# Attention's first group of q and k assembled by ScalarE instead of SBUF transfers, and the constant rows of the second buffer copied by a transfer

## The chip, the cores and the metric

The kernel runs on one core of a Trainium2 chip. A core has TensorE (PE, with its weight load PEld), VectorE (DVE), ScalarE (ACT), GpSimd (POOL) and SyncE (SP), which run their own instruction queues in order and wait for each other through semaphores. Transfers are issued by SP, ScalarE or GpSimd and carried by 16 DMA engines. The metric is device time in microseconds of one execution; lower is better. The times before are three runs, and one further execution was profiled.

## What is computed

The reference computes causal attention with a bias for 8 batches of 8 heads (576 positions, 64 wide), and sends each of the 4608 rows through one of 8 experts with a capacity of 576 rows each.

```python
scores = scale * np.matmul(q, k.transpose(0, 1, 3, 2))
s_pos = np.maximum(s, 0.0)
cum = np.cumsum(s_pos, axis=-1)
bias = -(cum[:, :, :, None] - cum[:, :, None, :])
scores = np.where(causal, -1000000000.0, scores + np.minimum(bias, 0.0))
scores = scores - np.max(scores, axis=-1, keepdims=True)
attn = np.exp(scores)
attn = attn / (np.sum(attn, axis=-1, keepdims=True) + 1e-09)
return np.matmul(attn, v).astype(np.float32)
...
x = np.ascontiguousarray(attn_out.transpose(0, 2, 1, 3)).reshape(B * S, H * D)
return _moe_ref(x=x, **moe_kwargs)
```

## The kernel before

Attention takes the first 309 us of the profiled execution; routing and the experts follow and depend on all of it. The 64 heads are worked on in 16 groups `g` of four heads. A group has two passes `pr`, and a pass two heads `par`, so there are 32 passes `n0 = 2*g + pr`.

Each group has one of four `QK` buffers, 128 partitions by two planes by q and k by two passes by 1280 columns. Values are carried in fp16 twice: `hi`, the scaled value rounded to fp16, and `lo`, what the rounding left. In plane 0, partitions 0 to 63 hold `hi`; partitions 64 to 69 are six extra rows with constants, the digits of the cumulated bias ("aux", line 416) and the row maxima. Plane 1 holds `hi` and `lo` one above the other on 128 partitions. `load` (line 384 on) builds a group:

- two loads each of q and k into `raw` (line 401), of which there are two buffers; the next group but one can be loaded when `raw` has been read;
- `hi` by ScalarE (line 428) and `lo` by VectorE (line 430), each on 128 partitions, into plane 1;
- six pieces `q2`, `k2`, `q3`, `k3`, `q4`, `k4` and two `e1` that bring 64-partition halves to the other half or plane. `move` (line 435) does this by a transfer from SBUF to SBUF of 72 KB for each pass; for the first group `e1` is a ScalarE activation from `raw` (line 438). The first group is done in two parts, one for each pass: 4 `e1` and 12 transfers.

The passes of a group then go through these steps:

- `spass` ("bound pass"): nine units of matmuls into `pss` (lines 505, 521; three PSUM buffers), each followed by a masked maximum on VectorE into `mr` (line 490). When all nine are done, two small activations (537, 539), a GpSimd subtraction (541), a transposition on TensorE (544) and an activation (546) make `mt`, and a transfer of 5 KB (549 on SP, 550 on ScalarE's queue) writes the maxima into partitions 67 and 68 of `QK`.
- `sts` ("score pass"): seven units of matmuls into `pst` (564 to 567, 607 to 609), the exponential by ScalarE (575) into `P`, and what bf16 leaves of it by GpSimd (577) into `R`. Its units need the maxima's transfer and all six pieces.
- `pv` (642 to 644): 90 small matmuls with V into `po`; then VectorE and ScalarE normalise (671, 675, 687 to 691), and `turn` transposes for the router (725, 744).

`consts` fills the six extra rows of all four `QK` buffers ahead of time: VectorE writes those of the buffers 0 and 1 (line 304), and GpSimd starts a transfer from buffer 1 to the buffers 2 and 3 (line 309).

The order of instructions is not written out. Every step is a task with an engine, an assumed duration, what it depends on and a priority `prio`. `Plan.run` is a list scheduler: over and over it takes, on the engine that is free first, the ready task of the lowest `prio`, by assumed durations, and emits it. A changed number thus moves instructions on all engines. The first `WARM` tasks on TensorE are matmuls on zeros (line 795, priority 50), which fill time until real ones are ready.

Of the kernel before, what the change touches and what calls it, by code (L numbers as in the profile page):

```python
# [27 lines left out]
QS = 32.0  # L28
# [10 lines left out]
PW = 1536  # L39
WARM, HALF = 70, 4  # L40

# [188 lines left out]
class Attention:  # L230
# [35 lines left out]
    def consts(self):  # L266
# [31 lines left out]
        for i in range(4):  # L298
            t = self.r["QK"].slots[i][0]
            p0 = -97 if i == 0 else 2 * i - 5.6  # L300
            rows, made = t[64:70, 0], []
            if i < 2:
                for c in (1, 0):
                    made.append(pl.add("v", 0.85, lambda rows=rows, c=c: nc.vector.tensor_scalar(
                        rows[:, c].rearrange("p r (h c) -> p (r h) c", h=2), zrow, self.vec[64:70, c:c + 1], None,
                        op0=OP.add), [k["vec", 0, 4], k["vec", 1, 1], k["mZ"]], prio=p0 if c or i else -94, lock=True))
            else:
# [4 lines left out]
            k["row", i] = made  # L312
            if i == 1:
                self.rows1, self.moved = made, []
# [67 lines left out]
    def load(self, g):  # L382
# [41 lines left out]
        for a, z in parts:  # L424
# [3 lines left out]
            hi = [pl.add("a", dur, lambda t=t, a=a, z=z: act(part(A_, 1, t, t, a, z), raw.t[:, t, a:z], AF.Copy, scale=QS),  # L428
                         [ld[r, t] for r in range(a, z)], prio=t0 - 5 + off + t / 10, uses=[raw, QK]) for t in range(2)]
            lo = [pl.add("v", 0.15 + n * S / 960, lambda t=t, a=a, z=z: stt(  # L430
                part(A_, 1, t, 1 - t, a, z), raw.t[:, t, a:z], QS, part(A_, 1, t, t, a, z), op0=OP.mult,
                op1=OP.subtract), [hi[t]], prio=t0 - 4.648 + off + t / 10, uses=[raw, QK], lock=True) for t in range(2)]

# [7 lines left out]
            else:  # L441
                e1 = [move((E_, 0, t, 0), (E_, 1, t, t), hi[t:t + 1], -4.4 + t / 20) for t in range(2)]
            q2 = move((E_, 0, 0, 1), (O_, 1, 0, 0), hi[:1], -4.3)
            k2 = move((E_, 0, 1, 1), (O_, 1, 1, 1), hi[1:], -4.25)
            q3 = move((O_, 1, 0, 0), (E_, 1, 0, 1), [lo[0], q2], -3.8)
# [7 lines left out]
    def vload(self, g):  # L453
        nc, pl, k = self.nc, self.pl, self.k
        b, hf = divmod(g, 2)
        t0, st = 2 * g, self.st[g]
        rv, V, Vl = self.buf("rv"), self.buf("V"), self.buf("Vl")
        st.update(V=V, Vl=Vl)
        ld = [pl.add("s", 0.45, lambda r=r: nc.sync.dma_start(rv.t[:, r], self.vN[b, :, 2 * hf + r]), prio=t0 - 4.5, uses=[rv],
                     kb=295, bulk=True) for r in range(2)]  # L460
        hi = pl.add("a", 0.2 + 2 * S / 1200, lambda: nc.scalar.activation(V.t[:, :, :, 0:64], rv.t, AF.Copy, scale=VS),
                    ld + ([k["V", g]] if g < 3 else []), prio=t0 - 1.852, uses=[rv, V])
        lo = pl.add("v", 0.15 + 2 * S / 960, lambda: nc.vector.scalar_tensor_tensor(
            Vl.t, rv.t, VS, V.t[:, :, :, 0:64], op0=OP.mult, op1=OP.subtract), [hi], prio=t0 - 0.677, uses=[rv, V, Vl], lock=True)
        st["v"] = (hi, lo)
# [12 lines left out]
    def spass(self, g, pr):  # L478
# [54 lines left out]
        def both():  # L533
# [15 lines left out]
        st["max", pr] = pl.add("s", 0.67, lambda: nc.sync.dma_start(to.t[67:69, 0, 0, pr], mt.t), [x], prio=n0 - 3.46,
                               uses=[mt, QK], kb=5, alt=("a", 0.62, lambda: nc.scalar.dma_start(  # L550
                                   to.t[67:69, 0, 0, pr], mt.t)) if n0 < 4 else None)

    def sts(self, g, pr):
# [17 lines left out]
        def unit(key, cols, dur, go, deps, prio):  # L571
            ps = self.buf("pst")
            c0, n = cols
            x = pl.add("t", dur, lambda: go(ps.t), ready + deps, prio=prio, uses=[ps, QK])
            e = pl.add("a", n / 1200 + 0.171, lambda: nc.scalar.activation(P.t[:, c0:c0 + n], ps.t[:, :n], AF.Exp, scale=1.0 / YS),  # L575
                       [x] + fresh, prio=prio + 0.645, uses=[ps, P])
            sub = lambda eng: eng.tensor_tensor(R.t[:, c0:c0 + n], P.t[:, c0:c0 + n], strided_hi(P.t)[:, c0:c0 + n],  # L577
                                                op=OP.subtract)
            r = pl.add("p", n / 547 + 0.1, lambda: sub(nc.gpsimd), [e] + fresh, prio=prio + 0.447, uses=[P, R], lock=True,
                       alt=("v", n / 960 + 0.16, lambda: sub(nc.vector)) if n0 == 4 * self.nb - 1 else None)  # L580
            st["e", pr][key] = (e, r)
        for m, (par, j) in enumerate(((0, 0), (0, 1), (0, 2), (1, 0), (1, 1), (1, 2))):
# [11 lines left out]
            else:  # L594
# [5 lines left out]
                dur = 4 * T_(64) + 2 * T_(256) + 4 * T_(128)  # L600
            unit((par, j), (par * PW + 512 * j, 512), dur, go, [], n0 + m * 0.139)

        def last(ps):

            for par in range(2):
# [3 lines left out]
                nc.tensor.matmul(ps[:, c:c + 64], self.identb, self.mU[:, c:c + 64], start=False, stop=True)  # L609
        unit("l", (2 * PW, 128), 6 * T_(64), last, [], n0 + 6 * 0.139)  # L610

    def pv(self, g, pr):
# [9 lines left out]
        for par in range(2):  # L622
# [3 lines left out]
            for i in range(5):  # L626
# [10 lines left out]
                def go(po=po, i=i, par=par, order=order, cs=cs):  # L637
                    H, o = strided_hi(P.t), po.t[:, 0:325].rearrange("p (i c) -> p i c", c=65)
                    for ki in order:
# [64 lines left out]
    def turn(self, g, pr):  # L704
# [12 lines left out]
        for i0, i1 in self.parts(2 * g + pr, 1):  # L717
# [949 lines left out]
```

## Time and profile before

| what | value |
|---|---|
| timed runs | 755.88, 757.05, 758.44 us; median 757.05 |
| profiled execution | 751.0 us, its span 749.2 us |
| PE busy | 713.6 us, 95% of the span |
| DVE busy | 587.9 us, 78% |
| ACT busy | 384.9 us, 51% |
| POOL busy | 350.2 us, 47% |
| granted TensorE clock, mean | 0.978 |

The span runs from the first to the last instruction of the execution. A share is an average over stages with different limits; in attention VectorE and TensorE are both busy nearly all the time, in the experts TensorE alone. A PE time is modelled, and contains some waiting.

### The profile page before, as it was taken

The numbers are of one execution on the slowest core, as the hardware profiler recorded it, in microseconds if no ns is written. First come the engines' busy times: TensorE is split into PE (matmuls) and PEld (weight loads), VectorE is DVE, ScalarE is ACT, GpSimd is POOL, SyncE is SP. The second block draws the span as 40 slices with busy tenths as digits, with TensorE's granted clock in tenths as the row PEclk, the third lists the DMA queues.
The fourth block names the chain that finished last, engine by engine and source line by source line (L and its number), as shares of the span: only waits on it lengthen the run. The fifth ranks groups of instructions, "written<-read, shape, count | busy, mean of one in ns | idle before, by whom it ended". The sixth has DMA issues, their size and how long they took to land.

```text
span 749.2 us, 22621 instructions
## 1 busy us (share of the span) xinstructions
PE 713.6 (95%) x8799; PEld 455.4 (61%) x8799; DVE 587.9 (78%) x1902; ACT 384.9 (51%) x793; POOL 350.2 (47%) x457
## 2 busy tenths in 40 slices
PE   7989999999999999747999999999999999999997
PEld 3567888887877888636645545545445454454544
DVE  9989999999999997878897968969789795450110
ACT  4478988888887887605334313333234342451111
POOL 6778888989888889502032050320312224201102
PEclk9999999999999999859999999999999999999999
DMA  6897878777658622206268384683837649931001
GB/s 192 204 219 219 229 204 233 200 206 213 161 172 257 173 74 83 66 7 217 68 185 210 113 171 133 196 220 114 225 100 188 188 159 222 292 113 43 23 15 50
DMA packets 90838, 119.00 MB, mean 159 GB/s; under 512 B 40350, under 2 KB 56862, under 8 KB 90718
## 3 DMA queue, kind: packets, MB, share of 16 engines
q1 hardware_dynamic: 84274, 98.16, 48.3%
q0 software_dynamic: 6000, 19.01, 8.6%
q8 instruction: 69, 1.13, 0.6%
q10 hardware_dynamic: 456, 0.39, 0.2%
q14 instruction: 39, 0.32, 0.1%
HBM read 71.68 MB, written 19.10 MB: 121 GB/s over the span
## 4 chain that ended last, share of the span: by engine, by line
PE 65%; issue 15%; DVE 7%; DMA 6%; POOL 4%; ACT 2%; SPq 0%; POOLq 0%; ACTq 0%; DVEq 0%
PE psm L1462 15%; PE psm L1568 14%; PE pst L564 5%; PE pst L565 5%; PE pss L521 4%; PE po L642 3%; PE po L644 3%; PE po L643 3%; PE pss L725 2%; PE psn L1466 2%; POOL out_dram L1521 2%; PE pss L505 2%; DVE pss L490 2%; PE pst L567 2%; PE psa L1139 1%
## 5 line engine op out<-in xcount | busy, mean ns | idle before, releaser
L577 POOL TENSOR_TENSOR R<-P 128x512 f16<-128x512 f32 (+1 forms) x220 | 221.7, 1035 | 23.6 <-ACT P L575 19.3
L1462 PE MATMUL psm<-xT,w1p 128*128 128x512 f16 (+1 forms) x876 | 194.0, 353 | 0.7 <-ACT xT L1404 0.7
L1568 PE MATMUL psm<-w2p,hT 128*128 128x512 f16 x744 | 168.8, 379 | 0.0
L1521 POOL DMA_INDIRECT out_dram<-y,ids x39 | 39.3, 1007 | 196.6 <-ACT y L1579 170.9
L1466 PE MATMUL psn<-xT,w1p 128*128 128x64 f16 x768 | 129.7, 193 | 0.0
L575 ACT ACTIVATE P<-pst 128x512 f32<-128x512 f32 (+1 forms) x224 | 116.9, 552 | 24.3 <-PE pst L565 11.0
L490 DVE CUSTOM_DVE_ANT_0 pss<-pss,mS 128x512 f32<-128x512 f32 (+3 forms) x256 | 122.4, 508 | 6.9 <-PE pss L521 4.5
L1462 PEld LDWEIGHTS <-w1p 128*128 128x128 f16 x876 | 79.2, 98 | 78.3 <-issue 0.8
L1568 PEld LDWEIGHTS <-hT 128*128 128x128 f16 x744 | 66.7, 98 | 75.6 <-issue 2.1
L564 PE MATMUL pst<-QK 70*128 70x64 f16 (+4 forms) x512 | 104.6, 246 | 1.2 <-DMA QK<-mt 0.8
L565 PE MATMUL pst<-QK 128*128 128x64 f16 (+4 forms) x512 | 103.9, 246 | 0.0
L644 PE MATMUL po<-V,R 128*128 128x65 f16 x945 | 102.0, 193 | 1.2 <-POOL R L577 1.2
L642 PE MATMUL po<-V,P 128*128 128x65 f16 x945 | 102.0, 195 | 0.0
L643 PE MATMUL po<-Vl,P 128*128 128x64 f16 x945 | 101.9, 192 | 0.0
L1384 POOL DMA_INDIRECT xg<-xs,ids x40 | 41.8, 1045 | 115.0 <-DVE ids L1341 41.5
L1482 ACT ACTIVATE hT<-psm 128x512 f16<-128x512 f32 x64 | 38.1, 596 | 107.0 <-PE psm L1462 87.3
L642 PEld LDWEIGHTS <-P 128*128 128x128 bf16 x960 | 89.4, 97 | 3.5 <-issue 0.2
L643 PEld LDWEIGHTS <-P 128*128 128x128 bf16 x960 | 88.9, 99 | 3.1 <-issue 0.6
L644 PEld LDWEIGHTS <-R 128*128 128x128 f16 x960 | 88.7, 97 | 1.3 <-POOL R L577 1.3
L1484 DVE SCALAR_TENSOR_TENSOR hT<-psm,hT 128x512 f16<-128x512 f32 x64 | 43.9, 688 | 39.5 <-ACT hT L1482 38.6
L521 PE MATMUL pss<-QK 67*128 67x384 f16 (+3 forms) x256 | 67.4, 301 | 7.0 <-DVE mr L490 4.2
L1579 ACT ACTIVATE y<-psm 128x512 f32<-128x512 f32 x31 | 18.5, 597 | 105.8 <-PE psm L1568 105.8
(253 smaller groups left out, 1469.0 us busy)
## 6 DMA issues: line engine op xcount, KB each, us to landing
QK<-QK SPq DMA_DIRECT2D x120, 144.0 KB
wst<-in_w_dram SPq DMA_DIRECT2D x32, 512.0 KB
wst<-in_w_dram SPq DMA_DIRECT2D x64, 256.0 KB
raw<-in_q_dram SPq DMA_DIRECT2D x32, 288.0 KB
raw<-in_k_dram SPq DMA_DIRECT2D x32, 288.0 KB
rv<-in_v_dram SPq DMA_DIRECT2D x32, 288.0 KB
xs<-xp SPq DMA_DIRECT2D x32, 256.0 KB
xs<-xp SPq DMA_DIRECT2D x8, 128.0 KB
```

Of the source, the lines that this page charges most:

```text
L490: return pl.add("v", dur, lambda: nc.vector.tensor_tensor_reduce(ps(), ps(), mask, 1.0, init() if init else -3e38, OP.add, OP.max, mr.t[:, ...
L521: nc.tensor.matmul(ps.t[:, :n], F()[:, q0:q0 + 128], F()[:, k0:k0 + n], start=True, stop=True)
L564: nc.tensor.matmul(ps[:, c0:c0 + n], F()[:, ks:ks + 128], F()[:, q:q + n], start=True, stop=False)
L565: nc.tensor.matmul(ps[:, c0:c0 + n], G()[:, ks:ks + 128], G()[:, q:q + n], start=False, stop=not diag)
L575: e = pl.add("a", n / 1200 + 0.171, lambda: nc.scalar.activation(P.t[:, c0:c0 + n], ps.t[:, :n], AF.Exp, scale=1.0 / YS), [x] + fresh, pri ...
L577: sub = lambda eng: eng.tensor_tensor(R.t[:, c0:c0 + n], P.t[:, c0:c0 + n], strided_hi(P.t)[:, c0:c0 + n], op=OP.subtract)
L642: nc.tensor.matmul(o[:, i], H[:, c:c + 128], V.t[:, pr, sl], start=f, stop=False)
L643: nc.tensor.matmul(o[:, i, 0:64], H[:, c:c + 128], Vl.t[:, pr, sl], start=False, stop=False)
L644: nc.tensor.matmul(o[:, i], R.t[:, c:c + 128], V.t[:, pr, sl], start=False, stop=l)
L1462: nc.tensor.matmul(ps[:, tiles[0]:tiles[-1] + 1] if len(tiles) > 1 else ps[:, tiles[0]], lhs(f, c, a), xT.t[:, tiles[0]:tiles[-1] + 1, 4 * ...
L1466: nc.tensor.matmul(pt.t[:, 64 * f:64 * f + 64], lhs(f, c, a), xT.t[:, 4, 4 * b + c, 0:64], start=s, stop=e)
L1568: nc.tensor.matmul(py.t, hT.t[:, f, a, 128 * i:128 * i + 128], w2p.t[:, f, b], start=f == 0 and k == 0, stop=f == 7 and k == 2)
```

## The change

For the first group all six pieces are made by ScalarE: `q2` and `k2` by activations straight from the upper half of `raw`, the others by activations from `QK` to `QK` that read one half of the partitions and write the other (`shift`, which takes the place of `move` for `g == 0`). The rows of buffer 1 are no longer written by VectorE; GpSimd now starts three transfers that copy the rows of buffer 0 to the buffers 1, 2 and 3, after the first group's aux rows have landed in it. Besides, `WARM` is 75 instead of 70, and most priorities have new numbers: a table `AHEAD` shifts those of the first two groups or passes, and the base values changed for all.

```diff
-WARM, HALF = 70, 4
+WARM, HALF = 75, 4
+AHEAD = dict(hi=(-0.679, -0.559, 0), lo=(0.448, 0, 0), vhi=(0, -0.745, 0), vlo=(0.394, 0, 0), s=(-0.22, 0, 0), mx=(-0.031, 0, 0), e=(-1.039, 0, 0), pv=(0, 0.03, 0))
...
-            if i < 2:
+            self.moved = {}
+            if i == 0:
                 for c in (1, 0):
                     made.append(pl.add("v", 0.85, lambda rows=rows, c=c: nc.vector.tensor_scalar(
...
-                made.append(pl.add("p", 0.9, lambda rows=rows: nc.gpsimd.dma_start(rows, self.r["QK"].slots[1][0][64:70, 0]),
-                                   self.rows1 + [k["QK", 1]], prio=-20, kb=62))
-                self.moved.append(made[0])
...
+        if g == 0:
+            self.moved = {i: pl.add("p", 0.9, lambda i=i: nc.gpsimd.dma_start(self.r["QK"].slots[i][0][64:70, 0], QK.t[64:70, 0]),
+                                    aux[0] + aux[1] + [k["QK", 0], k["QK", i]], prio=-30 + i, kb=62, uses=[QK]) for i in range(1, 4)}
...
+            def shift(to, fr, deps, o):
+
+                def go(a=a, z=z):
+                    act(part(*to, a, z), fr(a, z) if callable(fr) else part(*fr, a, z), AF.Copy, scale=QS if callable(fr) else 1.0)
+                return pl.add("a", dur, go, deps, prio=t0 + o + off, uses=[raw, QK] if callable(fr) else [QK])
+            if g == 0:
+                q2, k2 = (shift((E_, 0, t, 1), lambda a, z, t=t: raw.t[64:128, t, a:z], [ld[r, t] for r in range(a, z)],
+                                -5.05 + t / 20) for t in range(2))
+                move = shift
+            else:
+                q2 = move((E_, 0, 0, 1), (O_, 1, 0, 0), hi[:1], -4.3)
+                k2 = move((E_, 0, 1, 1), (O_, 1, 1, 1), hi[1:], -4.25)
...
-            prio = n0 - 2.847 + m * 0.082
+            prio = n0 - 2.651 + AHEAD["s"][min(n0, 2)] + m * 0.082
...
-            unit((par, j), (par * PW + 512 * j, 512), dur, go, [], n0 + m * 0.139)
+            unit((par, j), (par * PW + 512 * j, 512), dur, go, [], n0 + m * 0.151)
```

VectorE at its 14th to 20th row, in the first 17 us; `QK_91` and `QK_92` are the buffers 0 and 1, `pss` with `mr_105` the bound pass of pass 0. Before:

```order
L430 SCALAR_TENSOR_TENSOR QK_91<-raw_87,QK_91 128x576 x2
L304 TENSOR_SCALAR QK_92<-mZ,vec 6x2560 x2
L430 SCALAR_TENSOR_TENSOR QK_91<-raw_87,QK_91 128x576
L490 ISA pss_121,mr_105<-pss_121,mS 128x256
L490 ISA mr_105 128x1
L430 SCALAR_TENSOR_TENSOR QK_91<-raw_87,QK_91 128x576
L490 ISA pss_122,mr_105<-pss_122,mS 128x128
```

The changed kernel at the same place (its lines are numbered some 3 to 7 apart):

```order
L427 SCALAR_TENSOR_TENSOR QK_91<-raw_87,QK_91 128x576 x2
L311 MEMSET QK_92 128x8x64
L427 SCALAR_TENSOR_TENSOR QK_91<-raw_87,QK_91 128x576 x2
L497 ISA pss_121,mr_105<-pss_121,mS 128x128
L497 ISA mr_105 128x1
L497 ISA pss_122,mr_105<-pss_122,mS 128x256
```

The two row fills of buffer 1 are gone, a memset that GpSimd had done stands there, and all four `lo` come ahead of the first maximum, which is now that of the other head.

ScalarE in the same stretch, from the first group's second part on; `QK_92<-raw_88` is `hi` of the second group, `mp`, `ms` and `mt` the maxima of pass 0. Before:

```order
L438 ACTIVATE QK_91<-raw_87 64x576 x2
L428 ACTIVATE QK_91<-raw_87 128x576 [waits DMAHW3_49]
L428 ACTIVATE QK_91<-raw_87 128x576
L438 ACTIVATE QK_91<-raw_87 64x576 x2
L435 DMA QK_91<-QK_91 64x576 [waits DMAHW2_49,Activation_49]
L428 ACTIVATE QK_92<-raw_88 128x2x576 [waits DMAHW5_49,DMAHW0_49]
L435 DMA QK_91<-QK_91 64x576 [waits DMAHW6_49,DMAHW1_49,DVE_49]
...
L428 ACTIVATE QK_92<-raw_88 128x2x576 [waits DMAHW4_49]
L435 DMA QK_91<-QK_91 64x576 [waits DMAHW7_49,DVE_49,Activation_49]
L537 ACTIVATE mp_110<-mr_105 128x10 [waits DVE_49,Pool_49]
...
L550 DMA QK_91<-mt_112 2x10x128 [waits DMAHW1_49,Activation_49]
```

The changed kernel:

```order
L425 ACTIVATE QK_91<-raw_87 128x576 x2
L443 ACTIVATE QK_91<-raw_87 64x576 x2
L435 ACTIVATE QK_91<-raw_87 64x576 x2
...
L443 ACTIVATE QK_91<-QK_91 64x576
L425 ACTIVATE QK_92<-raw_88 128x2x576
L443 ACTIVATE QK_91<-QK_91 64x576
L425 ACTIVATE QK_92<-raw_88 128x2x576
L443 ACTIVATE QK_91<-QK_91 64x576 x2
L544 ACTIVATE mp_110<-mr_105 128x10
L546 ACTIVATE ms_108<-mr_105 128x10
L443 ACTIVATE QK_91<-QK_91 64x576 x2
L553 ACTIVATE mt_112<-pst_124 20x128
```

Where "..." stands, the pairs of lines 443 and 435 come once more, for the second part. Up to `mp` there are now eight activations of line 443 and no transfer of line 435; the maxima's transfer has left this queue.

That transfer is now issued by SP, as its 28th row, behind three loads for the third group and four moves of the second. It waits there for GpSimd's three copies of the rows, because it overwrites two of the six rows that they read.

TensorE in a later pass (11 of 0 to 31), after its first score unit; `pss` from `QK_93` are bound units of pass 12. Before:

```order
L567 MATMUL pst_126<-mT,identb 128x128
L505 LDWEIGHTS QK_93
L505 MATMUL pss_121<-QK_93 128x512
L505 LDWEIGHTS QK_93
L505 MATMUL pss_121<-QK_93 128x512
L564 LDWEIGHTS QK_92
L564 MATMUL pst_125<-QK_92 128x64
```

The changed kernel:

```order
L574 MATMUL pst_125<-mT,identb 128x128
L528 LDWEIGHTS QK_93
L528 MATMUL pss_123<-QK_93 128x512
L528 LDWEIGHTS QK_93
L528 MATMUL pss_121<-QK_93 128x256
L528 LDWEIGHTS QK_93
L528 MATMUL pss_122<-QK_93 128x512
L571 LDWEIGHTS QK_92
L571 MATMUL pst_126<-QK_92 128x64
```

One bound unit of two matmuls stood between the score units, and now three units stand there, one for each `pss` buffer. From pass 4 on such a run of three is found in nine passes of the changed kernel and in six of the kernel before.

## Rows read from the trace of the kernel before

**Rows 1.** Busy time by stretch: us, PE, PEld, DVE, ACT, POOL, PEclk, DMA share, GB/s.

```profile
10.00:28.40 18.40, 15.14 (x72) 6.74 (x70) 17.34 (x51) 7.82 (x14) 10.36 (x28) 0.91 0.76 189
28.40:60.00 31.60, 28.51 (x476) 21.88 (x475) 29.21 (x99) 23.61 (x54) 23.86 (x34) 1.00 1.00 237
60.00:110.00 50.00, 49.07 (x949) 40.27 (x949) 48.66 (x159) 43.48 (x104) 44.04 (x45) 1.00 0.78 216
110.00:195.00 85.00, 84.58 (x1649) 69.71 (x1647) 82.60 (x260) 72.30 (x170) 76.22 (x79) 1.00 0.76 214
195.00:251.00 56.00, 53.47 (x1025) 43.48 (x1022) 53.64 (x174) 46.53 (x108) 47.70 (x50) 1.00 0.64 178
```

**Rows 2.** Timeline of DVE, 4 to 28: start, us, line, operation, [idle before].

```profile
4.20 0.48 DVE L317 MEMSET QK<- 128x512 uint32 x1
...
9.57 1.41 DVE L430 SCALAR_TENSOR_TENSOR QK<-raw,QK 128x576 f16<-128x576 f32 x2
11.01 2.77 DVE L304 TENSOR_SCALAR QK<-mZ,vec 6x2560 f16<-6x2560 f16 x2
...
21.99 0.33 DVE L490 CUSTOM_DVE_ANT_0 pss<-pss,mS 128x128 f32<-128x128 f32 x1
...
23.15 1.35 DVE L430 SCALAR_TENSOR_TENSOR QK<-raw,QK 128x1152 f16<-128x1152 f32 x1
...
27.68 0.14 DVE L490 DVE_READ_ACCUMULATOR2_ANT mr<- 128x1 f32 x1
```

**Rows 3.** Timeline of ACT and its queue ACTq, 9 to 24.5.

```profile
10.29 1.25 ACT L438 ACTIVATE QK<-raw 64x576 f16<-64x576 f32 x2 [0.35 <-issue]
...
12.60 0.67 ACT L438 ACTIVATE QK<-raw 64x576 f16<-64x576 f32 x1
...
13.17 0.67 ACT L438 ACTIVATE QK<-raw 64x576 f16<-64x576 f32 x1
13.74 1.15 ACT L428 ACTIVATE QK<-raw 128x1152 f16<-128x1152 f32 x1
...
22.23 0.21 ACT L537 ACTIVATE mp<-mr 128x10 f16<-128x10 f32 x1 [2.64 <-DVE mr L490]
...
23.67 0.27 ACT L546 ACTIVATE mt<-pst 20x128 f16<-20x128 f16 x1 [1.13 <-PE pst L544]
23.96 0.70 ACTq L550 DMA_DIRECT2D QK<-mt  x1
```

**Rows 4.** Timeline of PE, 11 to 28.5.

```profile
11.90 0.49 PE L521 MATMUL pss<-QK 67*128 67x256 f16 x3 [0.57 <-DMA QK<-xp]
...
27.87 0.22 PE L521 MATMUL pss<-QK 67*128 67x128 f16 x1 [0.46 <-DVE mr L490]
...
28.47 0.38 PE L564 MATMUL pst<-QK 70*128 70x512 f16 x1
```

**Rows 5.** Waits of PE, 28.4 to 110: us in total, times, longest.

```profile
PE pss L521 <- DVE po L687: 1.1, 1, 1.1
PE pst L564 <- DMA QK<-mt: 0.8, 1, 0.8
...
PE pss L521 <- ACT mt L546: 0.7, 1, 0.7
```

**Rows 6.** Waits of DVE, 28.4 to 110.

```profile
DVE wgp L348 <- DMA wgf<-in_w_gate_dram: 1.5, 1, 1.5
```

**Rows 7.** Transfers issued up to 60: count, KB each, median us to landing.

```profile
QK<-QK SPq DMA_DIRECT2D x7, 72.0 KB
QK<-QK ACTq DMA_DIRECT2D x5, 72.0 KB
...
QK<-QK POOLq DMA_DIRECT2D x2, 60.0 KB, 5.0
```

**Rows 8.** An activation elsewhere that reads partitions 64 to 127 and writes 0 to 63.

```profile
L1584 ACT ACTIVATE t<-psm 64x512 f32<-64x512 f32 x8 | 4.8, 594 | 15.6 <-PE psm L1561 15.6
```

**Rows 9.** Waits of PE, 110 to 300.

```profile
PE pss L521 <- DVE mr L490: 0.9, 2, 0.7
```

More of the change, by code (lines that the diff above doesn't have):

```diff
@@ L305, in consts @@
                         rows[:, c].rearrange("p r (h c) -> p (r h) c", h=2), zrow, self.vec[64:70, c:c + 1], None,
-                        op0=OP.add), [k["vec", 0, 4], k["vec", 1, 1], k["mZ"]], prio=p0 if c or i else -94, lock=True))
-            else:
-                made.append(pl.add("p", 0.9, lambda rows=rows: nc.gpsimd.dma_start(rows, self.r["QK"].slots[1][0][64:70, 0]),
-                                   self.rows1 + [k["QK", 1]], prio=-20, kb=62))
-                self.moved.append(made[0])
-            k["row", i] = made
-            if i == 1:
-                self.rows1, self.moved = made, []
+                        op0=OP.add), [k["vec", 0, 4], k["vec", 1, 1], k["mZ"]], prio=-97 if c else -94, lock=True))
             x = t.rearrange("p a t r c -> p (a t r) c")[:, :, S:OH]
@@ L404, in load @@
         fresh = [k["QK", g]] if g < 4 else []
-        if g == 1:
-            fresh = fresh + self.moved
+        if g in self.moved:
+            fresh = fresh + [self.moved[g]]
         if g == 0:
@@ L428, in load @@
             hi = [pl.add("a", dur, lambda t=t, a=a, z=z: act(part(A_, 1, t, t, a, z), raw.t[:, t, a:z], AF.Copy, scale=QS),
-                         [ld[r, t] for r in range(a, z)], prio=t0 - 5 + off + t / 10, uses=[raw, QK]) for t in range(2)]
+                         [ld[r, t] for r in range(a, z)], prio=t0 - 5.237 + AHEAD["hi"][min(g, 2)] + off + t / 10, uses=[raw, QK]) for t in range(2)]
             lo = [pl.add("v", 0.15 + n * S / 960, lambda t=t, a=a, z=z: stt(
                 part(A_, 1, t, 1 - t, a, z), raw.t[:, t, a:z], QS, part(A_, 1, t, t, a, z), op0=OP.mult,
-                op1=OP.subtract), [hi[t]], prio=t0 - 4.648 + off + t / 10, uses=[raw, QK], lock=True) for t in range(2)]
+                op1=OP.subtract), [hi[t]], prio=t0 - 4.648 + AHEAD["lo"][min(g, 2)] + off + t / 10, uses=[raw, QK], lock=True) for t in range(2)]
             def move(to, fr, deps, o):
@@ L461, in vload @@
         hi = pl.add("a", 0.2 + 2 * S / 1200, lambda: nc.scalar.activation(V.t[:, :, :, 0:64], rv.t, AF.Copy, scale=VS),
-                    ld + ([k["V", g]] if g < 3 else []), prio=t0 - 1.852, uses=[rv, V])
+                    ld + ([k["V", g]] if g < 3 else []), prio=t0 - 1.852 + AHEAD["vhi"][min(g, 2)], uses=[rv, V])
         lo = pl.add("v", 0.15 + 2 * S / 960, lambda: nc.vector.scalar_tensor_tensor(
-            Vl.t, rv.t, VS, V.t[:, :, :, 0:64], op0=OP.mult, op1=OP.subtract), [hi], prio=t0 - 0.677, uses=[rv, V, Vl], lock=True)
+            Vl.t, rv.t, VS, V.t[:, :, :, 0:64], op0=OP.mult, op1=OP.subtract), [hi], prio=t0 - 0.677 + AHEAD["vlo"][min(g, 2)], uses=[rv, V, Vl], lock=True)
         st["v"] = (hi, lo)
@@ L537, in spass @@
         a1 = pl.add("a", 0.21, lambda: nc.scalar.activation(mp.t[:, 0:10].rearrange("p (a b) -> p a b", a=2), both(), AF.Copy, scale=1.0 / YS), done + fresh,
-                    prio=n0 - 3.46, uses=[mr, mp])
+                    prio=n0 - 3.025 + AHEAD["mx"][min(n0, 2)], uses=[mr, mp])
         a2 = pl.add("a", 0.21, lambda: nc.scalar.activation(ms.t.rearrange("p (a b) -> p a b", a=2), both(), AF.Copy, scale=1.0 / YS), done,
-                    prio=n0 - 3.46, uses=[mr, ms])
-        p1 = pl.add("p", 0.2, lambda: nc.gpsimd.tensor_sub(mp.t[:, 10:20], ms.t, mp.t[:, 0:10]), [a1, a2], prio=n0 - 3.46, lat=0.35,
+                    prio=n0 - 3.025 + AHEAD["mx"][min(n0, 2)], uses=[mr, ms])
+        p1 = pl.add("p", 0.2, lambda: nc.gpsimd.tensor_sub(mp.t[:, 10:20], ms.t, mp.t[:, 0:10]), [a1, a2], prio=n0 - 3.025 + AHEAD["mx"][min(n0, 2)], lat=0.35,
                     uses=[ms, mp])
@@ L544, in spass @@
         x = pl.add("t", 0.06, lambda: nc.tensor.transpose(ps.t.bitcast(F16)[:, 0:128], mp.t, self.ident16),
-                   [p1, k["i16b"]], prio=n0 - 3.46, uses=[ps, mp])
-        x = pl.add("a", 0.25, lambda: nc.scalar.activation(mt.t, ps.t.bitcast(F16)[0:20, 0:128], AF.Copy), [x], prio=n0 - 3.46,
+                   [p1, k["i16b"]], prio=n0 - 3.025 + AHEAD["mx"][min(n0, 2)], uses=[ps, mp])
+        x = pl.add("a", 0.25, lambda: nc.scalar.activation(mt.t, ps.t.bitcast(F16)[0:20, 0:128], AF.Copy), [x], prio=n0 - 3.025 + AHEAD["mx"][min(n0, 2)],
                    uses=[ps, mt])
         to = QK
-        st["max", pr] = pl.add("s", 0.67, lambda: nc.sync.dma_start(to.t[67:69, 0, 0, pr], mt.t), [x], prio=n0 - 3.46,
+        st["max", pr] = pl.add("s", 0.67, lambda: nc.sync.dma_start(to.t[67:69, 0, 0, pr], mt.t), [x], prio=n0 - 3.025 + AHEAD["mx"][min(n0, 2)],
                                uses=[mt, QK], kb=5, alt=("a", 0.62, lambda: nc.scalar.dma_start(
@@ L575, in unit @@
             e = pl.add("a", n / 1200 + 0.171, lambda: nc.scalar.activation(P.t[:, c0:c0 + n], ps.t[:, :n], AF.Exp, scale=1.0 / YS),
[L576 removed]
+                       [x] + fresh, prio=prio + 0.617 + AHEAD["e"][min(n0, 2)], uses=[ps, P])
             sub = lambda eng: eng.tensor_tensor(R.t[:, c0:c0 + n], P.t[:, c0:c0 + n], strided_hi(P.t)[:, c0:c0 + n],
@@ L609, in last @@
                 nc.tensor.matmul(ps[:, c:c + 64], self.identb, self.mU[:, c:c + 64], start=False, stop=True)
-        unit("l", (2 * PW, 128), 6 * T_(64), last, [], n0 + 6 * 0.139)
+        unit("l", (2 * PW, 128), 6 * T_(64), last, [], n0 + 6 * 0.151)
     def pv(self, g, pr):
@@ L665, in den @@
         nc, pl = self.nc, self.pl
-        prio = 2 * g + pr + 1.25 + 0.5 * par
+        prio = 2 * g + pr - 0.774 + 0.5 * par
         to, o = lambda: den.t[:, 0, par, a:z, None], lambda: po.t[:, 0:325].rearrange("p (i c) -> p i c", c=65)[:, a:z, 64:65]
@@ L675, in over @@
         return self.pl.add("v", 0.185, lambda: self.nc.vector.reciprocal(den.t[:, 1, p0:p1, a:z], den.t[:, 0, p0:p1, a:z]), x,
-                           prio=2 * g + pr + 1.25 + 0.5 * p0 - 1.423, uses=[den])
+                           prio=2 * g + pr - 0.774 + 0.5 * p0 + 0.338, uses=[den])
     def norm(self, g, pr, par, po, a, z, den, xp, x):
@@ L681, in norm @@
         b, hf = divmod(g, 2)
-        prio = 2 * g + pr + 1.25 + 0.5 * par
+        prio = 2 * g + pr - 0.774 + 0.5 * par
         h = 256 * hf + 128 * pr + 64 * par
@@ L746, in turn @@
             x = self.dots = pl.add("t", 0.059 * m * (1 if end else 2), dots, (out if end else [y for h in self.held for y in h[1]]) + [
-                k["gate"], self.dots] + free, prio=prio + 0.702, uses=[xt] if end else [h[0] for h in self.held],
+                k["gate"], self.dots] + free, prio=prio + 2.656, uses=[xt] if end else [h[0] for h in self.held],
                                     bank=self.bank[bank])
```

4 lines of the change are left out of this document (1 added, 3 removed).

## Prediction

> **What bounds the kernel now.** I read the busy time by stretch first, then the first 28 us engine by engine, then the waits. From 28.4 us on attention is full: from 110 to 195 TensorE is busy 84.58 of 85 us and VectorE 82.60, and even from 28.4 to 60, with the DMA engines at a share of 1.00, VectorE has 29.21 of 31.60 [rows 1]. What routing and the experts do starts when attention ends, so time is won in two ways: the first score unit starts earlier, or one of the few waits after it goes. The reader should see how small the second store is: PE is idle 3.09 us from 28.4 to 60, 0.93 from 60 to 110, 0.42 from 110 to 195 and 2.53 from 195 to 251 [rows 1], 7.0 us in all.
>
> The first score unit runs at 28.47. It is not a transfer that holds it: the matmul ahead of it, a bound unit of pass 2, waited for VectorE's `mr` [rows 4], and VectorE finished the bounds of pass 1 at 27.68 and was busy 17.34 of 18.40 us up to there [rows 1, 2]. So the start is a chain on VectorE: `lo` of the first part (9.57), the row fills of buffer 1 (11.01, 2.77 us), the other `lo`, nine maxima of pass 0, two `lo` of the second group, nine maxima of pass 1 [rows 2].
>
> **The row fills.** VectorE loses 2.77 us and gets a memset, 0.48 by its row: 2.29 saved, on that chain [rows 2]. After the first `lo` (end 11.0) the memset ends at 11.5, and two more `lo` at 0.7 each (1.41 for two) at 12.9. The second maximum then needs both `e1`. ScalarE's activations follow each other every 0.57 (12.60 to 13.17) [rows 3]; from 10.29 two `hi`, two pieces and two `e1` of the first part end at 10.29 + 5 x 0.57 + 0.67 = 13.8. The nine maxima of a pass take 27.68 - 21.99 - 1.35 = 4.34 us of VectorE, from pass 1 with its `lo` taken out [rows 2]. Pass 0 is thus done at 18.2, where 21.99 stands now. Two `lo` (2.7) end at 20.9 and pass 1 at 25.2, 2.5 us before the 27.68.
>
> **The pieces on ScalarE.** Twelve transfers of 72 KB go (seven on SP, five on ScalarE's queue) [rows 7], 0.86 MB; at the 237 GB/s of 28.4 to 60 [rows 1] that is 3.6 us of the DMA engines. Three copies replace two, so 60 KB come back. ScalarE gets twelve activations of 64x576. The trace has none that goes from `QK` to `QK` across partitions. Bounds: the one without a shift takes 0.67 alone and 0.57 in a row [rows 3]; the one that reads partitions 64 to 127 and writes 0 to 63 takes 0.594 for 512 elements, 0.67 scaled to 576 [rows 8], so the shift costs nothing. I take 0.57, as they stand in a row. ScalarE had room: 7.82 busy of 18.40 us [rows 1].
>
> But it is a queue. Up to the second `hi` of the second group stand twelve short activations and one `hi`: 10.29 + 12 x 0.57 + 1.15 = 18.3, and that `hi` ends at 19.5 [rows 3]. VectorE wants it at 19.5, after one `lo` from 18.2: nothing to spare. `mp` follows two pieces later, at 20.6 where 22.23 stands now. From `mp` to `mt` it is 1.44 us now [rows 3], within which the next two pieces fit, so `mt` starts at 22.1 and its transfer is issued at 22.4 instead of 23.96.
>
> [...]
>
> **The maxima's transfer.** Bounds of its landing: a tiny transfer issued on ScalarE at 9.68 was there for the matmul at 11.90 (its row is the one that PE waited for) [rows 4], near 2.2 us; the maxima's own, issued at 23.96, landed by 28.47, at most 4.5 [rows 3, 4]. So 24.6 to 26.9. With VectorE ready at 25.2, I take the first score unit at 26.4: **-2.1 us**, bounds -3.0 and -1.3 where all goes as above.
>
> It now waits for the row copies. GpSimd could start them when its last iota is over at 12.3 and two memsets of 0.95 are done, near 14.2; they land 5.0 us after issue by the median [rows 7], one behind the other near 19 to 21. That is hidden while it is under 22.4; each microsecond beyond holds the score units, and SP, behind which the loads of the third group stand.
>
> **After the start.** Three of PE's waits up to 110 come from late transfers: for the maxima of pass 1 (0.8), for `mt` behind a load of k (0.7), and 1.1 for `po` [rows 5], which follows VectorE's 1.5 us wait for the router's weights [rows 6]; SP now issues those weights 14 rows sooner. With 3.6 us less on the DMA engines I expect half of these 2.6 us to go: **-1.3 us**, bounds 0 and -2.6.
>
> **New numbers for all later passes.** Units change places on all engines. The stall that is left there is small (PE's idle 0.42 of 85 us), so little can be won: at most 3 us with the 2.53 from 195 to 251. What can be lost is not bounded by a row. I take 0, with -1.5 and +4 as ends. The five more warm matmuls run before there is real work and cost nothing.
>
> **Sum.** -2.1 - 1.3 + 0 = -3.4 us. For the profiled execution that is 751.0 - 3.4 = 747.6 (span 749.2 to 745.8). The median of the runs, 757.05, stands 6.05 above the profiled execution; I take that as unchanged: 753.6.
>
> **Rivals.**
> - *ScalarE's queue or the copies eat the start.* If the pieces run at 0.67 each, as alone [rows 3], the second `hi` ends 12 x 0.10 = 1.2 us later, VectorE waits for it, and `mp` comes at 22.0, no earlier than now. The same result if the third copy lands past 24. The start is then won by 0 to 1 us and the rest half: -1.0, 756.0. For it: the queue has no slack. Against: 0.57 is measured in just such rows. Chance 0.24. [...]
> - *Later passes improve too.* Most of the 7.0 us of idle time goes: -6, 751.0. For it: a few large waits make it up. Against: one of them is 1.5 us of a router step in the midst of attention that the change leaves alone, and TensorE's 99.5% leaves nothing elsewhere. Chance 0.12.
> - *Later passes get worse; slower than before.* Bound units now stand three in a row more often, one for each `pss` buffer. A unit whose buffer VectorE has not emptied stops all of TensorE behind it, score units included. Such a wait is 0.9 us for two now, the longest 0.7 [rows 9]. Over the 27 passes from pass 5 on, 0.13 us a pass would undo the gain and 0.21 us make the kernel slower by 0.3%. At 0.25 it is +6.8 - 3.4 = +3.4, 760.4. For it: VectorE is at 97% and has no reserve; against: nine runs of three, not 27, and six stood there already. Chance 0.17.
> - *The forecast*, between -2.3 and -5: 0.47.
>
> **Numbers.** 0.3% of 757 is 2.3 us, about what a measurement of this kernel can tell from no change. Faster: 0.47 and 0.12, less 0.04 for a forecast that just falls short, 0.55; within 0.3%: 0.24 and these 0.04, and 0.02 of the last rival, 0.30; slower 0.15. The range goes from 750.0, past the second rival's 751.0, to 759.5, short of the third's 760.4; what it leaves out I put at 2 in 10.
>
> **What the profile after would show.** Right: no row fill of buffer 1 on VectorE; the end of pass 0's bounds near 18 and of pass 1's near 25; activations of 64x576 every 0.57 us; the first score unit between 25.5 and 27.2; the wait for the router's weights gone; 110 to 195 as full as now. Wrong: a wait of VectorE's `lo` for ScalarE near 19.5; the maxima's transfer issued after 24, held by the copies; more PE waits for `mr` between 60 and 300. The prediction is wrong as a whole if the later passes move by more than the start.

## The result, and the profile after

Timed side by side, the changed kernel takes 759.51 us (22 runs) and the one before 755.48 (22 runs): ratio 1.0051, 95% interval 1.0033 to 1.0070, some 4 us slower. A second comparison (`after_again`) gave 1.0059 (1.0034 to 1.0085). The profiled execution after is 758.47 us, its span 756.6.

Busy time by stretch after, columns as in [rows 1]:

```profile
10.00:28.40 18.40, 14.81 (x69) 6.50 (x66) 16.06 (x49) 17.76 (x28) 9.45 (x27) 0.91 0.78 221
28.40:60.00 31.60, 27.49 (x399) 20.52 (x400) 28.26 (x95) 21.29 (x51) 23.69 (x30) 0.95 0.86 215
110.00:195.00 85.00, 84.05 (x1614) 68.32 (x1613) 81.81 (x261) 70.42 (x168) 74.96 (x79) 1.00 0.75 212
```

From 28.4 to 60 TensorE is a microsecond less busy, VectorE too, and the clock is 0.95 where it was 1.00. DMA's share fell to 0.86, as less traffic would have it, without a gain.

ScalarE, 9 to 24 us, answers to [rows 3]:

```profile
16.68 0.68 ACT L443 ACTIVATE QK<-QK 64x576 f16<-64x576 f16 x1
17.39 1.16 ACT L425 ACTIVATE QK<-raw 128x1152 f16<-128x1152 f32 x1
18.57 0.68 ACT L443 ACTIVATE QK<-QK 64x576 f16<-64x576 f16 x1
19.28 1.16 ACT L425 ACTIVATE QK<-raw 128x1152 f16<-128x1152 f32 x1
20.46 1.39 ACT L443 ACTIVATE QK<-QK 64x576 f16<-64x576 f16 x2
21.88 0.21 ACT L544 ACTIVATE mp<-mr 128x10 f16<-128x10 f32 x1
...
23.49 0.27 ACT L553 ACTIVATE mt<-pst 20x128 f16<-20x128 f16 x1
```

VectorE (first row: the memset in the fills' place; then the end of pass 0's bounds), SP's queue, and TensorE:

```profile
11.03 0.48 DVE L311 MEMSET QK<- 128x512 uint32 x1
...
14.46 0.43 DVE L497 CUSTOM_DVE_ANT_0 pss<-pss,mS 128x256 f32<-128x256 f32 x1 [0.86 <-PE pss L528]
...
19.96 2.62 DVE L427 SCALAR_TENSOR_TENSOR QK<-raw,QK 128x1152 f16<-128x1152 f32 x2
...
27.05 0.14 DVE L497 DVE_READ_ACCUMULATOR2_ANT mr<- 128x1 f32 x1
```

```profile
20.25 0.76 SPq L395 DMA_DIRECT2D raw<-in_q_dram  x1
22.19 0.59 SPq L410 DMA_DIRECT2D QK<-auxk  x2
22.83 0.36 SPq L395 DMA_DIRECT2D raw<-in_k_dram  x1
23.30 1.26 SPq L432 DMA_DIRECT2D QK<-QK  x2
24.77 0.71 SPq L556 DMA_DIRECT2D QK<-mt  x1
```

```profile
27.49 0.38 PE L802 MATMUL po<-mZ 128*128 128x512 f16 x1
29.07 0.49 PE L528 MATMUL pss<-QK 67*128 67x256 f16 x3 [1.21 <-DMA QK<-QK]
29.39 0.38 PE L571 MATMUL pst<-QK 70*128 70x512 f16 x1
```

The last fence is the start's answer: TensorE waits 1.21 us at a bound unit of pass 2, which stands ahead of the first score unit and needs the second group's moves. SP issued two of these at 23.30, behind the aux rows, before which it had stood still from 21.01 to 22.19. The first score unit runs at 29.39, not 28.47 [rows 4] or earlier.

SP's own waits, 15 to 30, name what it stood still for:

```profile
SPq L410 <- DMA QK<-QK: 1.1, 1, 1.1
```

This is GpSimd's first copy of the constant rows, started at 14.05: the semaphore that the aux rows wait for had its last update at 22.17. The forecast had the copies done by 19 to 21.

Waits of TensorE and of VectorE, 28.4 to 110 (us in total, times, longest), answer to [rows 5, 6]:

```profile
PE pss L528 <- DVE mr L497: 3.5, 8, 1.2
PE pss L528 <- DMA QK<-QK: 1.2, 1, 1.2
PE pst L571 <- ACT P L582: 0.5, 1, 0.5
```

```profile
DVE den L682 <- ACT den L678: 2.6, 2, 1.4
DVE L L761 <- POOL R L584: 1.0, 1, 1.0
```

The four late transfers of before are gone, and others stand in their place: TensorE for VectorE's maxima, VectorE for `den`.

### The profile page after: what moved, and what is told of

It is laid out like the page before. It is cut to its first block, busy times and chain, and to the rows that moved or that the text cites. A ratio compares the mean times of both kernels' runs of the same rounds, so it can differ in the third digit from the quotient of the medians.

```text
span 756.6 us, 22639 instructions
## 1 busy us (share of the span) xinstructions
PE 718.0 (95%) x8804; PEld 457.7 (60%) x8804; DVE 586.9 (78%) x1900; ACT 390.8 (52%) x805; POOL 347.2 (46%) x458
## 4 chain that ended last, share of the span: by engine, by line
PE 54%; issue 19%; DVE 17%; POOL 5%; ACT 3%; DMA 2%; POOLq 0%; another core or an unknown queue 0%; ACTq 0%; SPq 0%; DVEq 0%
PE psm L1469 12%; PE psm L1575 12%; DVE pss L497 5%; PE pst L571 3%; PE pst L572 3%; PE pss L528 3%; PE po L649 3%; PE po L651 3%; PE po L650 2%; POOL out_dram L1528 2%; PE pss L732 2%; DVE QK L427 2%; PE psa L1146 2%; PE psn L1473 2%; PE pss L512 1%
## 5 line engine op out<-in xcount | busy, mean ns | idle before, releaser
L584 POOL TENSOR_TENSOR R<-P 128x512 f16<-128x512 f32 (+1 forms) x221 | 217.4, 1010 | 25.3 <-ACT P L582 23.3
L649 PE MATMUL po<-V,P 128*128 128x65 f16 x945 | 107.5, 196 | 0.1
L651 PE MATMUL po<-V,R 128*128 128x65 f16 x945 | 107.4, 194 | 0.0
L650 PE MATMUL po<-Vl,P 128*128 128x64 f16 x945 | 107.3, 193 | 0.0
L528 PE MATMUL pss<-QK 67*128 67x512 f16 (+3 forms) x256 | 70.2, 303 | 9.6 <-DVE mr L497 4.2
## 6 DMA issues: line engine op xcount, KB each, us to landing
raw<-in_q_dram SPq DMA_DIRECT2D x32, 288.0 KB
raw<-in_k_dram SPq DMA_DIRECT2D x32, 288.0 KB
rv<-in_v_dram SPq DMA_DIRECT2D x32, 288.0 KB
```

The costliest lines, as they stand in the source:

```text
L528: nc.tensor.matmul(ps.t[:, :n], F()[:, q0:q0 + 128], F()[:, k0:k0 + n], start=True, stop=True)
L649: nc.tensor.matmul(o[:, i], H[:, c:c + 128], V.t[:, pr, sl], start=f, stop=False)
L650: nc.tensor.matmul(o[:, i, 0:64], H[:, c:c + 128], Vl.t[:, pr, sl], start=False, stop=False)
```

## How the runs are read

Two single profiles of one kernel differ by several us in the experts (after attention's last exponential, at 306.9 and 307.5, `before` takes 442.3 us and `before_again` 446.4), so I read attention by itself: the time at which TensorE has begun its 13,000th, 49,000th, 97,000th and 550,000th column of matmuls other than warm ones (summed over the records; all kernels have 1,542,042). "Half" is time at a granted clock of one half (1.2 GHz) between 20 and 100 us.

| kernel | 13,000 | 49,000 | 97,000 | 550,000 | 13 to 49 | 97 to 550 | half | ratio to before |
|---|---|---|---|---|---|---|---|---|
| before | 30.6 | 51.1 | 74.6 | 289.5 | 20.5 | 214.8 | 0 | |
| before_again | 30.8 | 53.0 | 76.2 | 290.1 | 22.3 | 213.9 | 3.4 | 0.9999 (0.9966 to 1.0033) |
| after | 31.4 | 53.2 | 77.0 | 293.5 | 21.8 | 216.5 | 3.4 | 1.0051 (1.0033 to 1.0070) |
| after_again | 31.3 | 53.1 | 77.0 | 293.5 | 21.8 | 216.5 | 3.4 | 1.0059 (1.0034 to 1.0085) |
| start_only | 32.6 | 53.5 | 81.0 | 294.8 | 20.9 | 213.8 | 10.2 | 1.0055 (1.0022 to 1.0088) |
| numbers_only | 32.2 | 54.9 | 80.8 | 295.9 | 22.8 | 215.1 | 0 | 1.0099 (1.0062 to 1.0136) |
| later_old | 31.0 | 52.5 | 76.5 | 294.0 | 21.5 | 217.5 | 0 | 1.0030 (1.0002 to 1.0058) |
| later_new | 30.8 | 55.8 | 79.9 | 294.7 | 25.0 | 214.8 | 6.8 | 1.0078 (1.0047 to 1.0110) |
| edit_old_order | 33.9 | 51.8 | 75.7 | 290.3 | 17.9 | 214.6 | 3.4 | 1.0023 (0.9996 to 1.0051) |
| old_edit_new_order | 35.8 | 58.3 | 81.6 | 298.3 | 22.5 | 216.8 | 4.0 | 1.0106 (1.0078 to 1.0134) |
| after_then_old | 30.2 | 52.1 | 76.7 | 291.5 | 21.9 | 214.8 | 3.4 | 1.0049 (1.0018 to 1.0079) |
| after_then_old_again | 30.3 | 50.8 | 79.7 | 294.7 | 20.5 | 215.0 | 6.8 | 1.0050 (1.0025 to 1.0075) |
| before_then_new | 30.8 | 50.3 | 82.1 | 298.3 | 19.5 | 216.2 | 6.8 | 1.0095 (1.0063 to 1.0127) |
| start20_then_old | 31.4 | 49.2 | 73.1 | 288.0 | 17.9 | 215.0 | 0 | 1.0007 (0.9971 to 1.0043) |
| start20_again | 34.5 | 55.9 | 79.8 | 294.7 | 21.5 | 214.9 | 13.6 | 1.0010 (0.9977 to 1.0043) |
| start30_then_old | 32.4 | 51.5 | 75.4 | 290.1 | 19.1 | 214.7 | 3.5 | 0.9981 (0.9953 to 1.0009) |
| rows_old_order | 33.5 | 56.6 | 80.5 | 295.8 | 23.1 | 215.4 | 17.1 | 1.0045 (1.0015 to 1.0075) |
| after_pv_ahead | 30.0 | 52.8 | 75.6 | 292.1 | 22.8 | 216.5 | 3.4 | 1.0047 (1.0020 to 1.0074) |
| after_score_first | 30.5 | 52.2 | 75.9 | 292.4 | 21.7 | 216.5 | 3.4 | 1.0049 (1.0029 to 1.0068) |
| start20_score_first | 32.4 | 50.3 | 74.2 | 288.3 | 17.9 | 214.1 | 0 | 1.0002 (0.9982 to 1.0023) |

## Experiments

**Edits and numbers apart.** `start_only` has both edits and all numbers of before, `numbers_only` the reverse. `later_old` is the changed kernel with the numbers of before for index 2 and up, `later_new` the kernel before with the new ones there, as in this line of `later_old`:

```diff
-            prio = n0 - 2.651 + AHEAD["s"][min(n0, 2)] + m * 0.082
+            prio = (n0 - 2.651 + AHEAD["s"][min(n0, 2)] + m * 0.082 if n0 < 2 else n0 - 2.847 + m * 0.082)
```

> Both edits of the first group (pieces by ScalarE, rows by three copies), with every number of the kernel before. Theory A, the new numbers of the later passes cost most: within 1.5 us of before. Theory B, the first group's edits cost it all, because score units of pass 1 start later and the rest only shifts: about 4 us slower than before, as the change is.

> All new numbers, with the first group's pieces by transfers and the rows filled as before. Theory A: about 3 us slower than before. Theory B: within 1.5 us of before.

> The changed kernel, but with the old numbers for every group and pass of index 2 and more. Theory A: within 1.5 us of before. Theory B: about 4 us slower, as the change.

> The kernel before, but with the new numbers for every group and pass of index 2 and more. Theory A: about 3 us slower than before. Theory B: within 1.5 us of before.

All four are slower, and the parts don't add up: the edits +0.55%, all numbers +0.99%, both together +0.51%. `start_only` lost what theory B had, `later_old` lies between the two, and `numbers_only` and `later_new` lost about twice what theory A had, so neither theory fits all four. The scheduler makes a new order for the whole of attention out of each of them; the comparison did not separate an edit from the order that follows it.

**The order written out.** So the emitted order was recorded and played back in place of the scheduler.

```diff
-        self.build()
-        self.pl.run()
+        self.build(); Plan.text = ORDER_TEXT
+        self.pl.run()
...
+    for i, (r, e, g) in enumerate(todo):
+        x = self.all[r]
...
+    self.start(self._when(x, e), x, e)
...
+free_run, Plan.run = Plan.run, replay
```

`edit_old_order` has both edits in the order of before, `old_edit_new_order` neither in the order of the changed kernel. `after_then_old` follows the changed kernel to the last exponential of pass 3 and then before, `before_then_new` the reverse; only the recorded order differs.

> The order of all instructions is that of the kernel before, written out; only the first group's pieces (now on ScalarE, at the places where their transfers were issued) and the row copies are the change's. Theory O (the order of the first 60 us costs, the edits themselves do not): as fast as before or faster by 1 to 2 us, ratio 0.997 to 1.000, first score unit near 27.5. Rival E (the edits cost by themselves, by ScalarE's queue or by the copies): slower by 3 to 4 us as with the old numbers (1.0055), first score unit near 29.3.

> The order of all instructions is that of the changed kernel, written out; the first group's pieces are transfers again and VectorE fills the rows of buffer 1. Theory O: slower than before, by 4 us or more (1.005 to 1.010), TensorE waiting near 36 us as in the changed kernel. Rival E: within 1.5 us of before (1.000 to 1.002).

> The changed kernel in its own order up to the end of pass 3 (some 65 us on the chip), what is left in the order of before. Theory O: it keeps the whole loss, 1.004 to 1.006. Rival L (the new order of the later passes costs): within 0.2% of before, 0.998 to 1.002.

> The kernel before in its own order up to the end of pass 3, what is left in the order of the changed kernel. Theory O: the same as before, 0.998 to 1.002. Rival L: slower by what the later order costs, 1.003 to 1.006.

`old_edit_new_order` (1.0106) does not price the order alone: it reaches 13,000 columns 5.2 us later than before. With the order of before the edits are within what can be told from no change (1.0023), though the start was far worse: the pieces stood where their transfers had been issued, VectorE waited 3.03 us for a `hi` behind them (16.0 to 19.0), and the first score unit came at 31.84. Of the 3.3 us lost at 13,000 columns 0.7 are left at 49,000. Its row for 28.4 to 60 shows how:

```profile
28.40:60.00 31.60, 30.03 (x453) 21.82 (x452) 31.35 (x110) 24.29 (x56) 24.27 (x35) 1.00 0.82 224
```

VectorE is busy 31.35 of 31.60 us. In this stretch VectorE sets the pace, and a later start shortens its waits.

`after_then_old` keeps the loss. From 97,000 to 550,000 columns, every execution with the later order of before takes 213.9 to 215.4 us, every one with that of the changed kernel 216.2 to 216.8: the later order costs 1.8 us by their means. `before_then_new` can't be read by its ratio: it loses some 8 us where the two orders meet, between 49,000 and 97,000 columns (TensorE waits 2.5 us for VectorE's `xp` there, and 6.8 us are at half clock), which neither kernel has.

**Only the start of the change.** `start20_then_old` has the changed kernel's order up to `mp` of pass 0, `start30_then_old` up to the last exponential of pass 0, both the order of before behind it. `rows_old_order` is before with the row copies alone:

```diff
-            if i < 2:
+            if i == 0:
...
+            self.moved = {i: pl.add("p", 0.9, lambda i=i: nc.gpsimd.dma_start(self.r["QK"].slots[i][0][64:70, 0], QK.t[64:70, 0]),
```

> The changed kernel in its own order up to the middle of the first group's pieces (pass 0's maxima), all that is left in the order of before. Theory V (VectorE sets the pace up to some 130 us, and what counts is how long it is without work; the edits take 2.3 us of work from it): attention ends 1 to 2.5 us earlier than before, ratio 0.997 to 0.999. Rival S (an earlier start is taken back, since the group loads and what follows them come no earlier): attention ends within 0.5 us of before, 0.999 to 1.001.

> As the last, with the changed kernel's order up to the end of pass 0 (some 34 us on the chip). Theory V: attention ends 1 to 2.5 us earlier than before, since the stalls of the changed kernel after 36 us are not in this order. If the order of the first 34 us is itself to blame for these stalls: 1 to 2 us later than before, ratio 1.001 to 1.003.

> Before in its own order, with the rows of buffer 1 copied by a transfer instead of filled by VectorE (three copies from buffer 0), pieces still transfers. Theory V: VectorE's 2.3 us show up in the end of attention, 1 to 2 us earlier than before. Rival S: nothing, within 0.5 us. If the copies hold the second group's aux rows: later by up to 1 us.

> The kernel before once more, against itself: ratio 0.998 to 1.002. If attention is as repeatable as kernels with one order suggest, its last exponential ends at 306.9 within 0.5 us, and the experts' part after it differs by several us from the 442.3 of the first profile.

Against 1.0049 of `after_then_old`, the only difference is the order between pass 0 and the end of pass 3: with that of before nothing is lost (1.0007, 0.9981). A gain over before, as Theory V had it, is not clear of the noise: both intervals contain 1. The row copies without the pieces lose 0.45%: near 26.3 TensorE waits 1.9 us for a transfer from `QK` to `QK`, then runs from 29.9 to 47.0 at half clock. Its timed runs, too, had a lower granted clock than those of before beside them, 0.9728 against 0.9773 on average.

**The suspects in that stretch, and repeats.** `after_pv_ahead` takes up the changed kernel's longest wait, on TensorE between products with V:

```profile
36.27 0.19 PE L649 MATMUL po<-V,P 128*128 128x65 f16 x1
...
37.84 0.52 PE L528 MATMUL pss<-QK 67*128 67x512 f16 x2 [1.22 <-DVE mr L497]
38.19 0.19 PE L649 MATMUL po<-V,P 128*128 128x65 f16 x1
```

Its edit is two bound units on TensorE, moved by some 75 rows; all other queues are unchanged:

```diff
-MATMUL pss_123<-QK_92 128x512
-MATMUL pss_121<-QK_92 128x256
...
+MATMUL pss_123<-QK_92 128x512
+MATMUL pss_121<-QK_92 128x256
```

> The changed kernel in its own order, but for two bound units of pass 3 on TensorE, which stand behind the products with V of pass 0 that they were ahead of. If the stall costs by itself: TensorE's wait of 1.2 us near 36.6 is gone, the first exponential of pass 1 comes 1 to 1.5 us earlier than 42.7, attention ends 1 us or more earlier than 311.3, ratio to before 1.003 to 1.004. If it is made up for later, or the lower clock is the cost: the end stays at 311 within 0.5 us, ratio 1.004 to 1.006.

> Once more the changed kernel up to the end of pass 3, then the order of before. By the traces the later order is 1.5 us of the loss: 1.002 to 1.004, some 1.5 us faster than the changed kernel beside it.

> The changed kernel once more, on the same chip as the three others: ratio 1.003 to 1.007, attention ends at 311.3 within 1 us.

> Once more the changed kernel's first 20 us and then the order of before. By the first trace (attention ends at 305.4) it is 0 to 2 us faster than before, 0.997 to 1.000, and 4 us or more faster than the changed kernel.

The first exponential of pass 1 comes at 41.05 instead of 42.72, and 550,000 columns are reached 1.4 us earlier. But this execution had its first score unit at 28.0, 1.4 us earlier than after, so that the gain was there before the moved units; from 13,000 to 49,000 columns it is slower (22.8) than any execution of the unmoved order (20.5 to 21.9), and TensorE waits at other places (1.1 for `P`, 1.0 for `mr`). So that wait is not the whole cause; whether it is a part, the timed runs can't tell (758.42 us, and 760.61 for `after_again` beside it).

The traces show another chain in this stretch that was not tried, here in the changed kernel:

```profile
56.02 1.16 ACT L425 ACTIVATE QK<-raw 128x1152 f16<-128x1152 f32 x1 [0.95 <-DMA raw<-in_k_dram]
57.09 0.16 ACT L678 ACTIVATE den<-po 128x5 f32<-128x5 f32 x1
57.28 0.22 DVE L682 RECIPROCAL den<-den 128x10 f32<-128x10 f32 x1 [1.15 <-ACT den L678]
57.80 0.38 PE L528 MATMUL pss<-QK 67*128 67x512 f16 x1 [0.59 <-DVE mr L497]
```

ScalarE's `hi` waits for its load of k with a `den` behind it, VectorE waits for that `den`, and TensorE for the maxima behind it on VectorE. In `after_again`, `after_then_old`, its repeat and `after_score_first` VectorE waits 1.59, 1.87, 3.02 and 1.05 us here, TensorE 1.02, 1.26, 2.41 and 0.43; in `after_pv_ahead` VectorE waits 0.53 and TensorE not at all. No execution with the order of before in this stretch has such a wait at this `den`. What it costs in the end no run shows.

The clock explains little of the loss: the timed runs had a mean granted clock of 0.9770 in `after_again` and 0.9783 in before beside it, but 0.9778 against 0.9783 in `after_then_old_again` and 0.9793 against 0.9789 in `after_score_first`, and all three are 0.5% or so slower.

`start20_again` reaches 550,000 columns 6.7 us later than its twin. Busy time of both, 24 to 30 and 30 to 44, the twin first:

```profile
24.00:30.00 6.00, 5.06 (x31) 2.30 (x29) 4.68 (x17) 2.45 (x6) 2.08 (x9) 1.00 0.59 146
30.00:44.00 14.00, 13.34 (x202) 9.90 (x201) 13.93 (x54) 10.93 (x26) 10.11 (x18) 1.00 0.69 177
```

```profile
24.00:30.00 6.00, 3.31 (x17) 1.40 (x16) 2.57 (x10) 1.37 (x3) 1.74 (x7) 1.00 0.61 142
30.00:44.00 14.00, 13.73 (x108) 8.92 (x108) 9.97 (x36) 7.31 (x15) 8.69 (x15) 0.51 0.35 84
```

In one, TensorE stood 0.59 us for a transfer near 28; in the other 2.7 us for the second group's moves, and then worked for 13.6 us at 0.51 of the clock. With equal instructions, that is more than the change costs.

**The start without that wait.** Both runs move the bound units of pass 2 that stood ahead of the first score unit behind the second score unit, one in each order; on TensorE, in the changed kernel's:

```diff
-MATMUL pss_121<-QK_92 128x256
-MATMUL pss_122<-QK_92 128x128
-MATMUL pss_123<-QK_92 128x384
...
+MATMUL pss_121<-QK_92 128x256
+MATMUL pss_122<-QK_92 128x128
+MATMUL pss_123<-QK_92 128x384
```

> The changed kernel in its own order, with the three bound units of pass 2 that stood ahead of the first score unit moved behind the first two score units. If the second group's moves held the start: the first score unit runs at 27.3 to 28.2 instead of 29.4, without a wait for a move; and since the order behind is the same, the end of attention moves by 1 us at most (310.5 to 311.4), ratio 1.003 to 1.006. If the start decides the end: attention ends 1.5 to 2 us earlier, ratio 1.002 to 1.003.

> The changed kernel's first 20 us, then the order of before, with the four bound units of pass 2 moved behind the first two score units. If the wait for the second group's moves is what lets TensorE's clock fall near 30 us in some executions: no stretch at half clock between 29 and 45, first score unit near 27.5, attention ends between 304.5 and 306.5, faster than before, 0.995 to 0.999. If VectorE or the loads set the pace in any case: 0.999 to 1.002.

```profile
PE pst L571 <- DMA QK<-mt: 0.9, 1, 0.9
```

In `after_score_first` TensorE's wait at the start is now for the maxima's transfer, and the first score unit runs at 28.14, 1.25 us earlier. The same rows without the edit give both: 29.39 and 29.27 in the two executions of the changed kernel, which waited 1.21 and 1.68 us for the moves, 29.71 in `start30_then_old` (2.14 us), and 28.20, 28.23 and 28.01 in `after_then_old`, its repeat and `after_pv_ahead`, which did not wait for them. So the moves hold the start in some executions only, in those of the changed kernel by some 1.2 us. At 550,000 columns 1.1 are left, and the ratio, 1.0049, does not tell it. `start20_score_first` kept full clock from 20 us on and is as fast as before (1.0002), not faster; its first score unit came at 29.15, not near 27.5, after 1.55 us of waiting for the maxima's transfer. No version was found that is faster than before beyond the noise.

## Why the prediction was wrong

The forecast was 753.6 us, the result 759.5; the time came out near the third rival's 760.4.

- *First score unit, -2.1: failed, +0.9.* One step that failed is the list of what it waits for: VectorE's bounds and the maxima's transfer were named, the second group's moves were not, though a bound unit of pass 2 already stood ahead of it in [rows 4]. They make up 1.2 of the 3.0 us between the forecast's 26.4 and 29.39, by the trace and `after_score_first`. The other 1.7, from 26.4 to 28.1, are the maxima's chain, in the next three points.
- *Pieces at 0.57 us: mis-sized.* They follow each other every 0.64 us from `raw` (11.56 to 12.84 for two) and 0.71 from `QK`. The second `hi` ends at 20.44, not 19.5, `mp` starts at 21.88, not 20.6, near the first rival's 22.0.
- *Pass 0's bounds done at 18.2: 19.96.* VectorE's work fell as said, but it then waited 0.86 us for a unit that needs the second `e1` (ScalarE had it at 14.10) and 0.66 for one that stood behind warm matmuls at half clock (14.6 to 18.0). The sign "`lo` waits for ScalarE" did not show, as both were late.
- *Maxima's transfer at 22.4: 24.77.* `mt` was ready at 23.8 instead of 22.4, which is 1.4 of the 2.4 us. For the other 1.0 SP was at the moves, behind the aux rows, which wait for the copy into their buffer. That copy, forecast for 19 to 21, was done at 22.17 and held SP for 1.1 us. In `after_again` and `after_then_old` it was done at 21.60 and 21.00, SP did not wait for it, and the maxima's transfer was issued at 24.46 and 24.34, so the late copy cost some 0.4.
- *Late transfers, -1.3: the waits went, the time did not.* The four rows of [rows 5, 6] are gone. What replaced them is longer: TensorE's waits from 28.4 to 110 are 5.5 us in all, 3.9 before.
- *New numbers, 0 with ends -1.5 and +4: here the time went, and this is the step that turned the sign.* The zero had no row behind it, as the forecast said of what can be lost. The order from pass 0 to the end of pass 3 costs 0.4% (1.0049 and 1.0050 against 1.0007, 1.0010 and 0.9981), some 3 us; beside each other, `after_then_old_again` took 759.96 us and `start20_again` 757.17. In the traces, at full clock, 13,000 to 49,000 columns take 20.5 us in it and 17.9 in the order of before with the same edits. The kernel before takes 20.5 there as well, so this is what the new order keeps the edits from winning. The order behind adds 1.8 us in the traces; the timed runs (1.0051 and 1.0059 against 1.0049 and 1.0050, the latter expected at 1.002 to 1.004) can't tell that from nothing.
- *The third rival was right in sign and wrong in place.* It put the loss in 27 passes from pass 5 on, at 0.25 us of waiting for `mr` each. TensorE waits for `mr` 0.7 us from 110 to 300, no more than the 0.9 of [rows 9].
- *That an earlier start passes on to the end* was the frame of the sum. In `edit_old_order` 2.6 of 3.3 us late were made up.

Open: which instructions of the new order between passes 0 and 3 cost it (the longest wait alone does not, the `hi` ahead of `den` was not tried), and how often the clock falls as in `start20_again`.

## What to carry to other kernels

Where priorities feed a list scheduler, an edit and its order are two changes: record the order, play it back with the edit alone, then splice the two orders to place the loss. Before pricing an earlier start, walk the queue of the waiting engine row by row: the instruction just ahead may wait for something that the edit leaves late. And ask which engine sets the pace behind the start, since it takes back what is won or lost there.

## What the runs showed that was not expected

One program had its first 50 us in two forms. With 3.4 us at half clock at 15.0 to 18.4, a run of warm matmuls ended 1.25 us later (at 23.09, against 21.84) and TensorE then waited little; without, it stood 0.72 us at 21.8 and 2.69 at 27.2, and half clock came in the real work, from 30.4 to 44.0. Stretches at half clock came in most executions of all kernels, and 13,000 to 49,000 columns took 1.3 us longer with one of 3.4 us (21.8 against 20.5 in the changed order).
